# The first nine blocks of a fused attention and feed-forward kernel in an order written by hand, and its last addition by halves

## The chip, the cores and the metric

The kernel runs on one NeuronCore of a Trainium2 chip. Its engines are TensorE (PE in the profile, with its weight loads as PEld), VectorE (DVE), ScalarE (ACT), GpSimd (POOL) and SyncE (SP), which here only issues DMAs. The metric is the time of one execution on the device in microseconds; lower is better.

## The reference

With S = 2048 tokens, D = 576 columns, 32 heads of 18 columns and a hidden width of 4608, all in float32:

```
xn  = layernorm(x)
qkv = xn @ wqkv                      # 576 x 1728
# each token attends to itself and the tokens 2, 4, ..., 14 before it (W = 8, dilation 2)
A   = softmax(q . k / sqrt(18)) . v  # per head
out = x + A @ wo + relu(xn @ w1) @ w2
```

## The kernel before

**Layout.** The tokens are split into two phases (ph), even and odd ones, because a token only attends to tokens of its own parity. A phase has eight tiles (i = 0 to 7) of 128 tokens; two neighbouring tiles make a token block (tb = 0 to 3) of 256.

**Products.** A float32 product is made of three products in the PE's fast format. Each operand is split into a high part (`hi`, a rounded copy made by ACT) and a low part (`lo` = operand - `hi`, made by DVE). `two` (line 143) does this for weights, `transpose_split` (line 266) for the transposed, normalized x, and `h_mm` for the hidden layer. The list `TERMS` (line 294) holds the 14 products of one result: four of high x with high w1, four of low x with high w1, the mixed last 64 columns (one with high, one with low w1), and four of high x with low w1.

**Slots.** The feed-forward part runs over slots n = (phase, chunk of three hidden blocks c, token block tb, hidden block f). `h_mm(n)` (line 467) makes one 128 x 256 piece of the hidden layer: 14 products, then the rectified high part by ACT (L476) and the low part by DVE (L477). `o_mm(n)` (line 482) multiplies it with w2: 12 products into two accumulators `po`, one for each tile; after the third block of a chunk DVE adds them onto x (L500), which is also where the result is kept until `done` (line 458) stores it. The main loop (line 579) runs `h_mm` two slots (`LAG`) ahead of `o_mm`.

**Loads and splits of weights.** `split_task` puts a load and a split into the deque `tasks`. `stage_more` (line 128) issues the load on SP into a buffer of the pool `stp` (four buffers), at most three ahead; `run_splits(n)` makes the splits due by slot n, in order, and each one lets the next load go. `HEADW` gives the slots at which the first three blocks of w1 and of w2 are due. SP issues its DMAs in order, and one that waits for a buffer holds up those behind it.

**The opening.** 24 transposes of the identity (`WARM`, line 104) occupy PE from the start. For every tile, `stats` (line 239) makes mean and variance on DVE (L245 to L247) and, on POOL, the negated mean `nm` (L249) and the reciprocal standard deviation `rstd` (L250). `norm` (line 254) makes `xn`, in one pass on DVE (L261) or, with `act`, in two on ACT (L258, L259); ACT then copies the last 64 columns a second time (L263), so that one transpose of 128 columns puts them on both halves of the partitions. `make_xt` (line 285) has PE transpose a tile (L275 four times, L276 once) and ACT and DVE split it into `xT` (L278 to L281). The table `HEAD` says after which slot the steps for tiles 2 to 7 are put. Each engine executes its instructions in the order in which they are written here, so this table and the loop set the queues of ACT and DVE.

**The middle.** The products for q, k and v (`qkv_tile`), the attention on DVE (queued in `bg` and taken in by `run_bg` as an estimate of DVE's and PE's progress, `t`, allows), and the product with wo (`wo_a` to `wo_b`) are woven into the slots. `UNIT0` = 7 is the slot of the first `qkv_tile`; the five parts of wq for it are split in slots 2 to 6.

**The end.** After the last `o_mm`, DVE adds each of the two accumulators onto its tile of 576 columns, and SP stores the two tiles.

Of the kernel before, what the change touches and what calls it, by code (L numbers as in the profile page):

```python
# [33 lines left out]
HEAD = (  # L34
    (-2, 0, 'stats', 3),
    (-2, 1, 'xt', 2, True),
    (-1, 0, 'stats', 4),
    (-1, 1, 'norm', 3, True),
    (0, 0, 'xt', 3, False),
    (0, 0, 'norm', 4, True),  # L40
    (0, 0, 'stats', 6),
    (0, 1, 'stats', 5),
    (1, 1, 'norm', 5, False),
    (1, 1, 'xt', 4, False),
    (2, 1, 'xt', 5, False),
    (2, 1, 'norm', 6, True),
    (2, 1, 'stats', 7),
    (4, 0, 'norm', 7, True),
    (4, 1, 'xt', 6, False),
    (5, 1, 'xt', 7, False),  # L50
)
HALO = ((0, 112), (112, 127))
WARM = 24
# [3 lines left out]
def tile_body(ctx: ExitStack, tc: tile.TileContext, x, wqkv, wo, w1, w2, out):  # L57
    nc = tc.nc
    S, D = x.shape
# [5 lines left out]
    KT = 4  # L65
    DR = D - KT * P
    D2 = D // 2
    scale = Dh ** -0.5
# [4 lines left out]
    pool = lambda name, bufs, **k: ctx.enter_context(tc.tile_pool(name=name, bufs=bufs, **k))  # L73
# [20 lines left out]
    f32 = lambda ap: ap.bitcast(F32)  # L94
# [18 lines left out]
    def mm(o, l, r, start, stop, n):  # L113
        nc.tensor.matmul(o, l, r, start=start, stop=stop)  # L114
        t["pe"] += n / 2400.0 + 0.002

    def dve(n):
        t["dve"] += (n + 130) / 960.0
# [16 lines left out]
    def run_splits(n):  # L135
        while staged and staged[0][0] <= n:
            _, split, st = staged.popleft()
            split(st)
            stage_more()

    held = None

    def two(hi, lo, src, n):
        def rest():
            nc.vector.tensor_tensor(lo, src, f32(hi), op=ALU.subtract)  # L145
            dve(n)

        nc.scalar.activation(hi, src, AF.Copy)  # L148
        if held is None:
            rest()  # L150
        else:
            held.append(rest)

    W1, W2, WQ, WO = {}, {}, {}, {}

# [83 lines left out]
    def stats(ph, i):  # L239
# [4 lines left out]
        for h in range(2):  # L244
            nc.vector.bn_stats(st[:, h, :], xt[:, h * D2 : (h + 1) * D2])  # L245
        nc.vector.bn_aggr(mv, st)
        nc.vector.tensor_scalar(mv[:, 1:2], mv[:, 1:2], EPS, None, op0=ALU.add)  # L247
        nm = smp.tile([P, 1], F32, name="nm", bufs=4)
        nc.gpsimd.tensor_scalar(nm, mv[:, 0:1], -1.0, None, op0=ALU.mult)  # L249
        nc.gpsimd.tensor_tensor(r, mv[:, 1:2], mhalf, op=ALU.pow)  # L250
        MR[ph, i] = nm, r
        dve(700)

    def norm(ph, i, act=False):
        nm, r = MR.pop((ph, i))
        xn = tmp.tile([P, 640], F32, name="xn", bufs=3)
        if act:
            nc.scalar.activation(xn[:, 0:D], X[ph, i], AF.Identity, bias=nm)  # L258
            nc.scalar.activation(xn[:, 0:D], xn[:, 0:D], AF.Copy, scale=r)  # L259
        else:  # L260
            nc.vector.tensor_scalar(xn[:, 0:D], X[ph, i], nm, r, op0=ALU.add, op1=ALU.mult)  # L261
# [4 lines left out]
    def transpose_split(src, last, hi, mix, lo, free=False):  # L266

        if free:
            pa, pb = (ps_o.tile([P, 2, 512], F32, name="po")[:, 0, :] for _ in range(2))
            pa, pb = pa.rearrange("p (k c) -> p k c", k=KT), pb[:, 0:P]  # L270
        else:
            pa = ps_m.tile([P, KT, P], F32, name="pm")
            pb = ps_m.tile([P, P], F32, name="pm")
        for k in range(KT):
            nc.tensor.transpose(pa[:, k, :], src[:, k * P : (k + 1) * P], ident)  # L275
        nc.tensor.transpose(pb, last, ident)  # L276
        t["pe"] += 5 * 0.06
        nc.scalar.activation(hi, pa, AF.Copy)  # L278
        nc.vector.tensor_tensor(lo, pa, f32(hi), op=ALU.subtract)
        nc.scalar.activation(mix, pb, AF.Copy)  # L280
        nc.vector.tensor_tensor(mix[DR:P], pb[DR:P], f32(mix[DR:P]), op=ALU.subtract)  # L281
        dve(512)
        dve(128)

    def make_xt(ph, i, free=False):
# [5 lines left out]
        transpose_split(xn[:, 0:512], xn[:, 512:640], d[:, 0:4, :], d[:, 4, :], d[:, 5:9, :], free)  # L291
# [175 lines left out]
    def h_mm(n):  # L467
        ph, c, tb, f = slots[n]
        w, xt = W1[ph, c, f], XT[ph, tb]
        pt = ps_h.tile([P, TBN], F32, name="ph")  # L470
        for j, (a, b) in enumerate(TERMS):
            wb = w[:, b // 5, (b % 5) * P : (b % 5 + 1) * P]
            mm(pt, wb, xt[:, a, :], j == 0, j == len(TERMS) - 1, TBN)
        hi = hp.tile([P, TBN], F32R, name="hhi")
        lo = hp.tile([P, TBN], F32R, name="hlo")
        nc.scalar.activation(hi, pt, AF.Relu)  # L476
        nc.vector.scalar_tensor_tensor(lo, pt, 0.0, f32(hi), op0=ALU.max, op1=ALU.subtract)  # L477
        t["dve"] = max(t["dve"], t["pe"] + 0.6)
        dve(TBN)
        H[n] = (hi, lo)  # L480

    def o_mm(n):
        ph, c, tb, f = slots[n]
        hi, lo = H.pop(n)
        w = W2[ph, c, f]
        for k in range(2):
# [3 lines left out]
            for j, (l, b) in enumerate(((hi, 0), (hi, 1), (lo, 0))):  # L490
                for h in range(2):
                    mm(
                        PO[k][:, h, 0:D2], l[:, cs], w[:, b, h * D2 : (h + 1) * D2],
                        f == 0 and j == 0, f == C - 1 and j == 2, D2,
                    )
        if f == C - 1:
            for k in range(2):
                i = 2 * tb + k
                acc = X[ph, i].rearrange("p (h c) -> p h c", h=2)
                nc.vector.tensor_tensor(acc, PO[k][:, :, 0:D2], acc, op=ALU.add)  # L500
                dve(D)
                if c == NCH - 1:
                    done(ph, i)


    todo = {}
# [50 lines left out]
    for i in range(1, AHEAD + 1):  # L557
        stage_more(i)
        load_x(0, 1 + i)
    for i in range(AHEAD + 2, NI):  # L560
        load_x(0, i)
    stats(0, 0)
    stats(0, 1)
    held = []
    run_splits(-5)
    norm(0, 0)
    norm(0, 1)
    stats(0, 2)
    make_xt(0, 0)
    make_xt(0, 1, True)  # L570
    for f in held:
        f()
    held = None
    run_splits(-LAG)
    norm(0, 2, True)
    for z, k, op, *a in HEAD:
        (late if k else at)(z, {"stats": stats, "norm": norm, "xt": make_xt}[op], 0, *a)
    M = (3.0, 1.5, 3.0)
    for n in range(-LAG, len(slots)):
        run_splits(n)  # L580
# [37 lines left out]
```

## Time and profile before

| | |
|---|---|
| median of three runs | 1184.16 us (1183.68 to 1187.38) |
| the profiled execution | 1184.46 us, of which the profile's span is 1182.7 us |
| mean granted clock of PE | 0.998 |
| busy time of DVE | 822.3 us (70%) |
| busy time of ACT | 306.9 us (26%) |
| busy time of POOL | 40.1 us (3%) |
| moved by DMA | 86.16 MB, mean 73 GB/s |

The span runs from the first to the last instruction of the profiled execution. A group of instructions is given by its line, engine and operation, the tile it writes and those it reads, its shape and count; then its busy time and the mean of one, and the idle time of its engine just ahead of it with what ended that. In the timeline, the first number is the start and the second the busy time of a row of equal instructions (`x4` is four of them). Matmuls overlap each other, so the pitch between them is shorter than the duration of one. L12 is line 12 of the kernel.

### The profile page before, as it was taken

Reading aid. Unit: us, or ns where it says so; the run is one execution under the profiler, and the core shown is the slowest. Engines: PE = TensorE matmul, PEld = TensorE weight load, DVE = VectorE, ACT = ScalarE, POOL = GpSimd, SP = SyncE. Lnnn points to the kernel's source line nnn. Section 1 sums busy time; section 2 is a strip of 40 time slices with the busy share of each in tenths; the row PEclk is TensorE's granted clock in tenths of the full one; section 3 lists DMA queues with packets and bytes.
Section 4 is the critical chain, followed back from the end, with each engine's and each line's share of the span. In section 5 each row is a group of like instructions: output and inputs, shape, how many; then the busy total and the mean of one; then the engine's idle time right before and its main releaser. Section 6 shows DMA issues by size and latency. Waiting matters only on the chain.

```text
span 1182.7 us, 21731 instructions
## 1 busy us (share of the span) xinstructions
PE 1174.6 (99%) x8936; PEld 1164.9 (98%) x8936; DVE 822.3 (70%) x1301; ACT 306.9 (26%) x758; POOL 40.1 (3%) x63
## 2 busy tenths in 40 slices
PE   8999999999999999999999999999999999999998
PEld 8999999999999999999999999999999999999998
DVE  7516885888687668877673288758777884787852
ACT  5422222131222211322233123121322222222210
POOL 2000000010000000000020000000100000000000
PEclk9999999999999999999999999999999999999999
DMA  5312121130312211356342122121302213114541
GB/s 174 85 32 79 39 84 47 47 108 1 99 45 58 65 55 44 104 112 148 105 131 74 47 55 80 32 77 27 98 21 80 70 43 89 47 30 110 115 100 60
DMA packets 137364, 86.16 MB, mean 73 GB/s; under 512 B 48832, under 2 KB 120768, under 8 KB 137264
## 3 DMA queue, kind: packets, MB, share of 16 engines
q1 hardware_dynamic: 134736, 76.58, 24.0%
q10 hardware_dynamic: 2528, 8.20, 2.4%
q8 instruction: 70, 1.15, 0.4%
q14 instruction: 30, 0.25, 0.1%
HBM read 66.58 MB, written 9.96 MB: 65 GB/s over the span
## 4 chain that ended last, share of the span: by engine, by line
PE 95%; DVE 2%; DMA 2%; ACT 0%; SPq 0%; issue 0%; POOL 0%; DVEq 0%; ACTq 0%
PE ph L114 37%; PE po L114 37%; PE pm L114 20%; DMA st<-in_w 1%; DMA xn<-turned 1%; PE pm L275 0%; DVE pr L382 0%; DMA turned<-tr 0%; DVE x L500 0%; DMA x<-in_x 0%; DVE pr L345 0%; SPq L424 0%; DVE w1t L145 0%; DVE w2t L145 0%; DVE bst L245 0%
## 5 line engine op out<-in xcount | busy, mean ns | idle before, releaser
L114 PE MATMUL ph<-xT,w1t 128*128 128x256 f32 x4032 | 513.0, 278 | 1.3 <-ACT xT L278 0.6
L114 PEld LDWEIGHTS ph<-xT,w1t 128*128 128x128 f32 x4032 | 491.9, 188 | 2.1 <-ACT xT L278 0.8
L114 PE MATMUL po<-w2t,hhi 128*128 128x288 f32 x2304 | 400.7, 296 | 0.6 <-DVE w2t L145 0.3
L114 PEld LDWEIGHTS po<-w2t,hhi 128*128 128x128 f32 x2304 | 336.9, 188 | 2.4 <-issue 0.5
L476 ACT ACTIVATE hhi<-ph 128x256 fp32r<-128x256 f32 x288 | 110.1, 382 | 553.5 <-PE ph L114 538.2
L114 PE MATMUL po<-w2t,hlo 128*128 128x288 f32 x1152 | 244.7, 293 | 0.0
L477 DVE SCALAR_TENSOR_TENSOR hlo<-ph,hhi 128x256 fp32r<-128x256 f32 x288 | 121.5, 422 | 161.0 <-ACT hhi L476 160.1
L500 DVE TENSOR_TENSOR x<-po,x 128x576 f32<-128x576 f32 x192 | 143.4, 756 | 69.9 <-PE po L114 67.0
L114 PE MATMUL pm<-wq,xT 128*128 128x432 f32 x896 | 185.5, 358 | 0.0
L114 PEld LDWEIGHTS po<-w2t,hlo 128*128 128x128 f32 x1152 | 183.6, 188 | 0.0
L114 PEld LDWEIGHTS pm<-wq,xT 128*128 128x128 f32 x896 | 163.8, 188 | 5.6
L145 DVE TENSOR_TENSOR w2t<-st,w2t 128x576 fp32r<-128x576 f32 x72 | 54.3, 755 | 45.6 <-ACT w2t L148 45.4
L345 DVE TENSOR_TENSOR pr<-qo,k 128x1152 f32<-128x1152 f32 x64 | 85.8, 1349 | 0.0
L348 DVE TENSOR_REDUCE lg<-pr 128x64 f32<-128x1152 f32 x64 | 84.9, 1343 | 0.0
L375 DVE TENSOR_TENSOR pr<-lg,v 128x1152 f32<-128x1152 f32 x64 | 84.7, 1350 | 0.2
L382 DVE TENSOR_TENSOR pr<-pr 128x288 f32<-128x288 f32 (+1 forms) x128 | 70.6, 601 | 0.1
L145 DVE TENSOR_TENSOR w1t<-st,w1t 128x640 fp32r<-128x640 f32 x72 | 59.0, 820 | 13.8 <-ACT w1t L148 13.7
L148 ACT ACTIVATE w2t<-st 128x576 fp32r<-128x576 f32 x72 | 49.1, 683 | 57.2 <-PE po L114 42.4
L314 ACT ACTIVATE k<-pm 128x144 f32<-128x144 f32 x64 | 18.6, 291 | 143.9 <-PE pm L114 143.9
L148 ACT ACTIVATE w1t<-st 128x640 fp32r<-128x640 f32 x72 | 53.0, 736 | 11.4 <-DMA st<-in_w 11.4
L351 POOL TENSOR_SCALAR_AFFINE_SELECT lg<-lg 1x512 f32<-1x512 f32 x8 | 9.4, 1171 | 844.1 <-DVE lg L348 844.1
L114 PE MATMUL pm<-wq,oT 128*128 128x288 f32 x224 | 35.2, 296 | 0.3 <-ACT oT L438 0.3
(61 smaller groups left out, 444.7 us busy)
## 6 DMA issues: line engine op xcount, KB each, us to landing
st<-in_w SPq DMA_DIRECT2D x72, 288.0 KB, 3.0
st<-in_w SPq DMA_DIRECT2D x72, 256.0 KB, 3.0
st<-in_wqkv SPq DMA_DIRECT2D x32, 216.0 KB, 3.0
turned<-tr SPq DMA_DIRECT2D x64, 80.0 KB, 2.3
xn<-turned SPq DMA_DIRECT2D x16, 320.0 KB, 3.2
st<-in_w SPq DMA_DIRECT2D x144, 32.0 KB, 2.7
out<-x SPq DMA_DIRECT2D x16, 288.0 KB, 2.1
x<-in_x SPq DMA_DIRECT2D x15, 288.0 KB, 3.6
```

The costliest lines, as they stand in the source:

```text
L114: nc.tensor.matmul(o, l, r, start=start, stop=stop)
L145: nc.vector.tensor_tensor(lo, src, f32(hi), op=ALU.subtract)
L148: nc.scalar.activation(hi, src, AF.Copy)
L314: nc.scalar.activation(k[:, W - 1 + i, :], pq[:, 1, :], AF.Copy)
L345: nc.vector.tensor_tensor(pr[i], q, window(k, i), op=ALU.mult)
L348: nc.vector.tensor_reduce(lg[:, i], pr.pop(i).rearrange(heads, d=Dh), axis=AX.X, op=ALU.add)
L351: nc.gpsimd.affine_select(out=z, in_=z, pattern=[[1, NI], [1, W], [0, HG]], compare_op=ALU.is_ge, fill=-1e9 / scale, base=1 - W, channel_m ...
L375: nc.vector.tensor_tensor(pr[i].rearrange(heads, d=Dh), e, window(v, i).rearrange(heads, d=Dh), op=ALU.mult)
L382: nc.vector.tensor_tensor(o, z[:, 0:n], z[:, n : 2 * n], op=ALU.add)
L476: nc.scalar.activation(hi, pt, AF.Relu)
L477: nc.vector.scalar_tensor_tensor(lo, pt, 0.0, f32(hi), op0=ALU.max, op1=ALU.subtract)
L500: nc.vector.tensor_tensor(acc, PO[k][:, :, 0:D2], acc, op=ALU.add)
```

## The change

The slots 0 to 3 of `o_mm` and 0 to 5 of `h_mm`, with all steps of tiles 0 to 5, are no longer made by the loop and the table `HEAD` but written out one after another; the loop begins at slot `FIRST` = 4. To that end `stats`, `transpose_split`, `h_mm` and `o_mm` can be called in parts. In detail:

- All splits of the first w1 and w2 blocks are placed ahead of token block 1. The three second products (`o_mm`) of token block 0 are made before `h_mm` of block 1 (`o_mm(0)`, `o_mm(1)`, tile 3's transposes, `o_mm(2)`, then `h_mm(3)`). `h_mm(0)` and `h_mm(1)` are interleaved by terms.
- SP's order of loads: w1 block 1 and 2 stand ahead of x 3, and the three blocks of w2 ahead of x 4 to 7. `stp` has five buffers instead of four.
- The low parts of the first two blocks of w1 and of the five parts of the first wq are made by POOL (`by_pool`) instead of DVE.
- Tile 0 is normalized by ACT, tiles 1 to 5 by DVE (before: 0, 1 and 5 by DVE, 2 to 4 by ACT). Tiles 6 and 7 stay on ACT.
- The last 64 columns are no longer copied twice, in either phase: PE transposes 64 columns, and DVE reads the same 64 rows again for the low part.
- In the last slot, each accumulator is filled one half of the columns after the other, DVE adds it in two halves of 288 columns, and each half is stored by a DMA of its own, from SP and ACT in turn.

```
-HEADW = (-5, -2, -1, 0, 0, 1)
+HEADW = (-9, -8, -7, -6, -5, -4)
+FIRST = 4
 HEAD = (
...
+    (4, 0, 'stats', 6),
+    (4, 1, 'norm', 6, True),
+    (4, 1, 'stats', 7),
+    (5, 0, 'norm', 7, True),
+    (5, 1, 'xt', 6),
+    (6, 0, 'xt', 7),
 )
...
-    stp = pool("stp", 4)
+    stp = pool("stp", 5)
...
     def two(hi, lo, src, n):
...
+        nc.scalar.activation(hi, src, AF.Copy)
+        if step_now in by_pool:
+            nc.gpsimd.tensor_tensor(lo, src, f32(hi), op=ALU.subtract)
+        else:
             nc.vector.tensor_tensor(lo, src, f32(hi), op=ALU.subtract)
             dve(n)
...
     def norm(ph, i, act=False):
...
-        nc.scalar.activation(xn[:, D:640], xn[:, KT * P : D], AF.Copy)
...
+        nc.tensor.transpose(pb, src[:, KT * P : D], ident)
...
+        def last_high():
+            nc.scalar.activation(mix[0:DR], pb, AF.Copy)
+
+        def last_low():
+            nc.vector.tensor_tensor(mix[DR:P], pb, f32(mix[0:DR]), op=ALU.subtract)
+            dve(128)
...
     def o_mm(n, out=True):
...
+            if end:
+                terms.sort(key=lambda z: z[3])
...
+    def o_out(n, which=range(2)):
...
+            for h in range(2):
+                nc.vector.tensor_tensor(acc[:, h], PO[k][:, h, 0:D2], acc[:, h], op=ALU.add)
+                (nc.scalar if h else nc.sync).dma_start(o_v[ph, i][:, h * D2 : (h + 1) * D2], acc[:, h])
...
+    by_pool.update((-9, -8, *range(UNIT0 - 5, UNIT0)))
+    both, x_low, w_low, last = TERMS[0:4], TERMS[4:8], TERMS[9:13], [TERMS[8], TERMS[13]]
     load_x(0, 0, 2)
     load_x(0, 1)
...
+    stage_more(1)
+    load_x(0, 2)
+    stage_more(4)
+    load_x(0, 3)
+    stage_more(5)
+    stats(0, 0)
+    norm(0, 0, True)
+    stats(0, 1)
+    norm(0, 1)
+    x0 = make_xt(0, 0, parts=True)
+    x0[0]()
+    run_splits(-9)
+    x1 = make_xt(0, 1, bank=ps_o, parts=True)
+    x1[0]()
+    x0[1]()
+    x1[1]()
+    h_terms(0, both)
+    run_splits(-8)
+    stage_more(4)
+    for i in range(4, NI):
         load_x(0, i)
...
+    stats(0, 2)
+    for z in x0[2:], x1[2:]:
+        for f in z:
+            f()
+    h_terms(0, x_low)
+    h_terms(1, both)
+    h_terms(1, x_low)
+    h_terms(0, w_low + last)
+    h_terms(1, w_low + last)
+    run_splits(-7)
+    norm(0, 2)
+    h_out(0)
+    run_splits(-6)
+    h_terms(2, TERMS, True)
+    h_out(1)
+    stats(0, 3)
     run_splits(-5)
...
+    h_out(2)
+    x2 = make_xt(0, 2, bank=ps_h, parts=True)
+    x2[0]()
+    x2[2]()
+    norm(0, 3)
+    run_splits(-4)
+    x2[1]()
+    x2[3]()
+    o_mm(0)
+    o_mm(1)
+    make_xt(0, 3, bank=ps_h)
+    o_mm(2, out=False)
+    stats(0, 4)
+    stats(0, 5)
+    h_mm(3)
+    norm(0, 4)
+    norm(0, 5)
+    h_terms(4, TERMS)
+    h4 = h_out(4, parts=True)
+    h4[0]()
+    o_out(2, (0,))
+    make_xt(0, 4)
+    o_out(2, (1,))
+    h4[1]()
+    h_terms(5, TERMS)
+    h5 = h_out(5, parts=True)
+    h5[0]()
+    make_xt(0, 5)
+    h5[1]()
+    o_mm(3)
...
-    for n in range(-LAG, len(slots)):
+    for n in range(FIRST, len(slots)):
```

In this, `h_terms(n, terms)` makes the named products of `h_mm(n)`, `h_out(n)` its high and low part, `o_out(n)` the additions of `o_mm(n)`; `make_xt(..., parts=True)` returns the four steps high, low, high of the last 64, low of the last 64 (`x0[0]` to `x0[3]`).

More of the change, by code (lines that the diff above doesn't have):

```diff
@@ L264, in norm, with transpose_split @@
         XN[ph, i] = xn
[L266 to L270, printed above, removed]
+    def transpose_split(src, hi, mix, lo, bank=None, parts=False):
+        if bank is ps_o:
+            po = ps_o.tile([P, 2, 512], F32, name="po")
+            pa, pb = po[:, 0, :].rearrange("p (k c) -> p k c", k=KT), po[0:DR, 1, 0:P]
@@ L286, in make_xt @@
+        def last_low():
+            nc.vector.tensor_tensor(mix[DR:P], pb, f32(mix[0:DR]), op=ALU.subtract)
+            dve(128)
+        steps = high, low, last_high, last_low
+        if not parts:
+            for f in steps:
+                f()
+        return steps
+    def make_xt(ph, i, bank=None, parts=False):
         tb, h = divmod(i, 2)
@@ L465, in tile_body, with h_terms, h_out, high @@
     H, PO = {}, {}
-    def h_mm(n):
+    HP, HN = {}, {}
+    def h_terms(n, terms, other=False):
         ph, c, tb, f = slots[n]
         w, xt = W1[ph, c, f], XT[ph, tb]
-        pt = ps_h.tile([P, TBN], F32, name="ph")
-        for j, (a, b) in enumerate(TERMS):
+        if n not in HP:
+            HP[n] = ps_m.tile([P, TBN], F32, name="pm") if other else ps_h.tile([P, TBN], F32, name="ph")
+            HN[n] = 0
+        for a, b in terms:
             wb = w[:, b // 5, (b % 5) * P : (b % 5 + 1) * P]
-            mm(pt, wb, xt[:, a, :], j == 0, j == len(TERMS) - 1, TBN)
+            HN[n] += 1
+            mm(HP[n], wb, xt[:, a, :], HN[n] == 1, HN[n] == len(TERMS), TBN)
+    def h_out(n, parts=False):
+        pt = HP.pop(n)
         hi = hp.tile([P, TBN], F32R, name="hhi")
         lo = hp.tile([P, TBN], F32R, name="hlo")
[L476 to L479, printed above, removed]
         H[n] = (hi, lo)
-    def o_mm(n):
+        def high():
+            nc.scalar.activation(hi, pt, AF.Relu)
+        def low():
+            nc.vector.scalar_tensor_tensor(lo, pt, 0.0, f32(hi), op0=ALU.max, op1=ALU.subtract)
+            t["dve"] = max(t["dve"], t["pe"] + 0.6)
+            dve(TBN)
+        if not parts:
+            high()
+            low()
+        return high, low
+    def h_mm(n):
+        h_terms(n, TERMS)
+        h_out(n)
+    def o_mm(n, out=True):
         ph, c, tb, f = slots[n]
@@ L485, in o_mm @@
         w = W2[ph, c, f]
+        end = n == len(slots) - 1
         for k in range(2):
```

122 lines of the change are left out of this document (49 added, 73 removed).

## The prediction

> **What bounds the kernel now.** I read the engines' busy time and the chain that ended last, on the page, and then the opening and the end, the only places where the change puts work in another order.
>
> ```profile
> PE 1174.6 (99%) x8936; PEld 1164.9 (98%) x8936; DVE 822.3 (70%) x1301; ACT 306.9 (26%) x758; POOL 40.1 (3%) x63
> ...
> PE 95%; DVE 2%; DMA 2%; ACT 0%; SPq 0%; issue 0%; POOL 0%; DVEq 0%; ACTq 0%
> ```
>
> TensorE (PE) works 99% of the span and is 95% of the chain. Little can be won in the middle; what counts is how much of PE's time at the two ends is not products. The chain in order of time gives the price of PE's work at full clock: one o_mm of 12 products, the five transposes of a tile (two rows), one h_mm of 14 products.
>
> ```profile
> 22.62 1.59 PE po L114 x12
> 24.21 0.44 PE pm L275 x4
> 24.65 0.11 PE pm L276
> 24.76 1.61 PE ph L114 x14
> ```
>
> The timeline (start, duration) gives two marks to count the opening between: the first transposes of tile 0, and h_mm(9), the first product of token block 3. From about there to the last slot every engine has the same order in both kernels, apart from some copies of ScalarE (ACT) that go away.
>
> ```profile
> 1.35 5.38 PE L105 MATMUL po<-ident 128*128 128x128 f32 x24 [1.35 <-POOL mhalf L99]
> 4.26 0.22 POOL L249 TENSOR_SCALAR nm<-mv 128x1 f32<-128x1 f32 x1 [2.92 <-DVE mv L246]
> 5.84 0.22 POOL L249 TENSOR_SCALAR nm<-mv 128x1 f32<-128x1 f32 x1 [0.75 <-DVE mv L246]
> 6.52 0.97 PE L275 MATMUL pm<-ident,xn 128*128 128x128 f32 x4
> 8.80 0.57 POOL L250 TENSOR_TENSOR rstd<-mv,mhalf 128x1 f32<-128x1 f32 x1
> ...
> 42.22 1.78 PE L114 MATMUL ph<-xT,w1t 128*128 128x256 f32 x14
> ```
>
> From 6.52 to 42.22 are 35.70 us. The work ahead of the second mark is nine h_mm, seven o_mm and the transposes of eight tiles, in both kernels: 9 x 1.61 + 7 x 1.59 + 8 x 0.55 = 30.0 us. So **5.7 us are lost in the opening**, the most that a new order can bring there. Part of it is the clock, as two windows show (length, then busy time of PE, its weight loads, VectorE (DVE), ACT and GpSimd (POOL), granted clock, DMA):
>
> ```profile
> 7.24:10.65 3.41, 2.09 (x14) 1.41 (x13) 3.25 (x9) 3.27 (x10) 0.75 (x2) 1.00 0.95 257
> 10.66:14.06 3.40, 3.40 (x16) 3.18 (x16) 2.16 (x5) 1.49 (x4) 0.00 (x0) 0.50 0.96 314
> ```
>
> PE was busy for 2.09 of 3.41 us, and the 3.40 us behind that ran at a granted clock of 0.50: half of it, 1.7 us, is lost. The other 4.0 us are waits.
>
> **The start, up to the first product.** The groups of instructions have the durations of all that follows (the number behind the comma is the mean of one in ns):
>
> ```profile
> L477 DVE SCALAR_TENSOR_TENSOR hlo<-ph,hhi 128x256 fp32r<-128x256 f32 x288 | 121.5, 422 | 161.0 <-ACT hhi L476 160.1
> L476 ACT ACTIVATE hhi<-ph 128x256 fp32r<-128x256 f32 x288 | 110.1, 382 | 553.5 <-PE ph L114 538.2 <-DMA k<-k 15.3
> L145 DVE TENSOR_TENSOR w1t<-st,w1t 128x640 fp32r<-128x640 f32 x72 | 59.0, 820 | 13.8 <-ACT w1t L148 13.7
> L145 DVE TENSOR_TENSOR w2t<-st,w2t 128x576 fp32r<-128x576 f32 x72 | 54.3, 755 | 45.6 <-ACT w2t L148 45.4
> L148 ACT ACTIVATE w1t<-st 128x640 fp32r<-128x640 f32 x72 | 53.0, 736 | 11.4 <-DMA st<-in_w 11.4
> L148 ACT ACTIVATE wq<-st 128x432 fp32r<-128x432 f32 (+1 forms) x50 | 29.1, 582 | 5.9 <-DMA st<-in_wo 3.2 <-DMA st<-in_wqkv 2.7
> L245 DVE BATCH_NORM_STATS2 bst<-x 128x6 f32<-128x288 f32 x32 | 13.1, 448 | 3.4 <-DMA x<-in_x 3.3
> L246 DVE BATCH_NORM_AGGREGATE mv<-bst 128x2 f32<-128x12 f32 x16 | 3.3, 209 | 0.6
> L247 DVE TENSOR_SCALAR mv<-mv 128x1 f32<-128x1 f32 x16 | 2.5, 154 | 0.6
> L249 POOL TENSOR_SCALAR nm<-mv 128x1 f32<-128x1 f32 x16 | 6.0, 372 | 166.3 <-DVE mv L246 166.3
> L258 ACT ACTIVATE xn<-x,nm 128x576 f32<-128x576 f32 x5 | 3.9, 775 | 0.0
> L261 DVE TENSOR_SCALAR xn<-x,nm,rstd 128x576 f32<-128x576 f32 x11 | 6.8, 621 | 0.9 <-POOL rstd L250 0.7
> L278 ACT ACTIVATE xT<-pm 128x512 fp32r<-128x512 f32 x14 | 8.3, 594 | 7.2 <-PE pm L275 7.1
> L279 DVE TENSOR_TENSOR xT<-pm,xT 128x512 fp32r<-128x512 f32 x14 | 9.6, 688 | 4.8 <-ACT xT L278 4.8
> L281 DVE TENSOR_TENSOR xT<-pm,xT 64x128 fp32r<-64x128 f32 x14 | 4.1, 295 | 0.4
> ```
>
> Tile 0's norm goes to ACT: from nm at 4.26 + 0.22 = 4.48, two passes (L258, and L259 over the same columns) of 0.78 end at 6.04. DVE would be quicker, but the warm-up transposes (1.35 + 5.38) hold PE until about 6.5, so it costs nothing; without that cover it would cost about 0.5. Tile 1: nm at 5.84 + 0.22, rstd 0.57 (the undisturbed row at 8.80), norm 0.62 on DVE, done at 7.25. Its transposes follow tile 0's at once and end near 7.9, since they no longer wait for the 64-column copies of L263. Then ACT stands in the way. It starts when tile 0's four transposes end (6.52 + 0.97 = 7.5) and does tile 0's high part, w1's, and tile 1's before the first product can go: 7.5 + 0.59 + 0.74 + 0.59 = 9.4. **PE idles 1.5 us**, and 0.2 more until tile 1's low part is there (9.4 + 0.69, against four products to do).
>
> **VectorE's queue.** From 9.4 on it holds, ahead of the transposes of tile 4: three low parts of 512 (0.688) and four of 64 rows (0.295), statistics of tiles 2 to 5 (2 x 0.448 + 0.209 + 0.154 = 1.26 each), one low part of w1 (0.82), three of w2 (0.755), four of h (0.422), norms of tiles 2 to 4 (0.62): 2.06 + 1.18 + 5.04 + 0.82 + 2.27 + 1.69 + 1.86 = 14.9, up to 24.3. Neighbours overlap a little:
>
> ```profile
> 28.43 0.60 ACT L278 ACTIVATE xT<-pm 128x512 fp32r<-128x512 f32 x1 [1.05 <-PE pm L275]
> 28.55 1.41 DVE L500 TENSOR_TENSOR x<-po,x 128x576 f32<-128x576 f32 x2
> ...
> 28.93 0.27 ACT L280 ACTIVATE xT<-pm 128x128 fp32r<-128x128 f32 x1
> ```
>
> Two adds of L500 take 1.41, where w2's low part over the same 576 columns takes 0.755 for one, and ACT's L280 starts 0.10 before L278 ends. Over some 18 such places on DVE that is up to 0.9, so the queue ends at 23.4 to 24.3. PE arrives there at 9.6 + 5 x 1.61 + 3 x 1.59 + 2 x 0.55 = 23.5 at full clock and waits 0 to 0.8; I take 0.4. The queue would be no shorter than before, had not two low parts of w1 (2 x 0.82) gone to POOL, since three norms (3 x 0.62) come to it from ACT.
>
> **POOL's low parts.** No run here shows a subtraction of this size on POOL. The bounds are its nearest rows:
>
> ```profile
> L306 POOL MEMSET k<- 1x1008 f32 x8 | 7.4, 931 | 0.0
> L351 POOL TENSOR_SCALAR_AFFINE_SELECT lg<-lg 1x512 f32<-1x512 f32 x8 | 9.4, 1171 | 844.1 <-DVE lg L348 844.1
> masks.py:199 POOL TENSOR_SCALAR_AFFINE_SELECT ident<-ident 128x128 f32<-128x128 f32 x1 | 0.3, 292 | 0.1
> ```
>
> The memset makes an element in 0.92 ns, the select in 2.29 (1171 for 512, 292 for 128). For 640 elements that is 0.59 to 1.46 us; a second input read behind the first would double the upper one to 2.9. I take 1.5, by the select, which reads and writes as this does. The first part (ACT is done with it at 8.8) is then ready at 10.3, the second at 11.8, while PE has 4 + 4 + 8 products to do before it needs them. nm and rstd of tile 2, queued behind on POOL, come at 12.6, about when DVE reaches that norm: cost 0. The five parts of wq (432 elements, 0.99 each) leave DVE too; the first three fill POOL for 3.0 us from the start of h_mm(6), and nm of tile 6 is wanted 1.61 + 0.38 + 0.42 + 1.10 = 3.5 after that start: 0.5 of cover.
>
> **The transposes of tile 7** wait for the buffer of tile 6's. From the end of h_mm(6): high and low of h (0.38 + 0.42), statistics (1.10), nm (0.37), norm 6 on ACT (1.55), wq's fourth high part (0.58), high of h (0.38), norm 7 (1.55), tile 6's high (0.59) and low (0.69) = 7.6; PE has two o_mm, two h_mm and one tile beside it, 6.95. A wait of 0.7, less ACT's four overlaps of 0.1: 0.3 taken, 0 to 0.7 possible.
>
> **The clock.** In the stretch that decided before, PE stood idle for 3.41 - 2.09 = 1.3 us. In the same stretch it will now be idle for the 1.5 us ahead of the first product, so I expect half clock in the next 3.4 us again. That costs 1.7, but brings PE to tile 4 behind the end of DVE's queue, so that of the 0.4 there 0.2 is left. The losses are 1.5 + 0.2 + 1.7 + 0.2 + 0.3 = 3.9 against 5.7: **the opening wins 1.8** (1.2 to 2.3 by the bounds of the two waits). The Trainium skill has another rule: by "TensorE: Matmul & The Clock Gate", Part 1, full clock is lost only after an idle window of some 3.4 us. PE never stood for that long here, so by that rule the clock would stay full, which is the first rival below; the rows above, half clock after a stretch with PE busy for 61%, disagree with it, and the rows decide.
>
> **What costs nothing:** the loads of x 4 to 7 stand on SyncE behind w2's third, which waits for POOL's first part, 10.3. One takes, from issue to landing,
>
> ```profile
> x<-in_x SPq DMA_DIRECT2D x15, 288.0 KB, 3.6
> ```
>
> and tile 4's statistics are 3.5 us ahead of the end of DVE's queue, at about 20: some 6 us of cover. The fifth staging buffer only lets w2's second load go before any split has freed one.
>
> **The end.** One last add behind the last product becomes two of 288, and the stores are halved:
>
> ```profile
> 1178.76 0.76 DVE x L500
> L453 DVE TENSOR_TENSOR x<-pm,x 128x288 f32<-128x288 f32 x32 | 13.1, 453 | 28.0 <-PE pm L114 28.0
> out<-x SPq DMA_DIRECT2D x16, 288.0 KB, 2.1
> ```
>
> In the built program the first half's add waits for the last product of the whole accumulator, not for its own half's, so nothing starts earlier. Two adds take 0.91, less their overlap, against 0.76. The last store has half the bytes; what that saves of 2.1 us no row shows, between nothing and, by bytes, 1.0. So -0.15 to +0.9. The two last stores share the engines, hence nearer to the lower end: **0.2 won**.
>
> **The sum.** The profiled execution took 1184.46 us (span 1182.7), 0.3 above the median of the runs, 1184.16. 1184.46 - 1.8 - 0.2 = 1182.5, by itself 1181.3 to 1183.4.
>
> **Rivals.** *Full clock.* If the throttle lets the next stretch run, the losses are 1.5 + 0.2 + 0.4 + 0.3 = 2.4: 3.3 won, 4.0 if both waits overlap away, 2.7 if rstd of tile 2 is held up by DVE, as here:
>
> ```profile
> 18.63 1.17 POOL L250 TENSOR_TENSOR rstd<-mv,mhalf 128x1 f32<-128x1 f32 x1
> ```
>
> (1.17 instead of 0.57, beside low parts of w2). With 0.2 to 0.9 for the end: 1181.6 to 1179.6, middle 1180.9. For it: the trace gives only one share after which the clock fell. Against: the new share is no higher. *POOL is the bound, slower.* The low parts take twice the select's rate, 2.9 us. nm and rstd of tile 2 come 2 x 1.4 = 2.8 later, and DVE's queue with them; three parts of wq take 5.9 instead of 3.0, so nm of tile 6 is 2.4 late. 1182.5 + 2.8 + 2.4 = 1187.7, less the 0.5 of waits that this swallows: 1187.2. It decides from about 2.2 us a part, where the opening's win is gone. Against: the select's rate; for: two inputs, and 1.5 leaves no cover at tile 2. *The written order stalls PE elsewhere*, by some 2 us: 1184.5, no change. Against: the covers above.
>
> **Chances.** Forecast 0.52, full clock 0.30, POOL 0.13, stalls elsewhere 0.05. A measurement of this kernel tells about 0.3%, 3.6 us: faster is below 1180.6, slower above 1187.7. Of full clock rather over half lies below 1180.6, if I allow for the range of its waits and for the runs' own spread: 0.18. Of POOL the dearer half lies above 1187.7: 0.07. The range, 1180.0 to 1186.0, leaves out some 8 in 100 below and 9 above.
>
> **What would show it.** Right: first product near 9.4; w1t on POOL near 1500 ns; a granted clock of 0.50 for 3.4 us before 15; short waits ahead of the transposes of tiles 4 and 7; h_mm(9) near 40.4. Wrong: w1t on POOL above 2.2 us, with tile 2's norm waiting for rstd; h_mm(9) at 42 or later; the last store landing more than 2.9 us (0.76 + 2.1) behind the last product.

## The result, and the profile after

The changed kernel takes 1181.72 us (median of 8 executions, 1181.18 to 1182.05), the kernel before 1184.80 beside it (8, 1183.68 to 1187.38). The ratio is 0.9971, with a 95% interval of 0.9962 to 0.9981: some 3 us are won, a small gain but clear of the noise. The forecast was 1182.5, range 1180.0 to 1186.0. The profiled execution took 1181.42 us.

Its page: the span, and the busy times (DVE 3.5 us less than before, ACT 5.0 less, POOL 7.4 more).

```profile
span 1179.7 us, 21695 instructions
PE 1171.0 (99%) x8936; PEld 1162.3 (99%) x8936; DVE 818.8 (69%) x1298; ACT 301.9 (26%) x738; POOL 47.5 (4%) x70
```

The opening, from the timeline of the changed kernel (start, busy time, engine, line; in brackets what ended the idle time). The lines have moved: L274 are the transposes, L105 all products, L260 the norm on DVE, L279 and L282 the high and the low part of a tile, L139 the low parts on POOL, L500 and L503 those of h.

```profile
6.16 0.66 PE L274 MATMUL pm<-ident,xn 128*128 128x128 f32 x4 [0.23 <-ACT xn L258]
7.08 0.58 DVE L260 TENSOR_SCALAR xn<-x,nm,rstd 128x576 f32<-128x576 f32 x1 [0.70 <-POOL rstd L245]
7.71 0.66 PE L274 MATMUL po<-ident,xn 128*128 128x128 f32 x4 [0.79 <-DVE xn L260]
8.51 0.60 ACT L279 ACTIVATE xT<-po 128x512 fp32r<-128x512 f32 x1 [0.44 <-PE po L275]
9.16 0.74 PE L105 MATMUL ph<-xT,w1t 128*128 128x256 f32 x4 [0.69 <-ACT xT L279]
...
12.82 1.82 PE L105 MATMUL pm<-xT,w1t 128*128 128x256 f32 x14
...
23.83 0.63 PE L274 MATMUL pm<-ident,xn 128*128 128x128 f32 x4 [0.17 <-DVE xn L260]
...
37.41 0.65 PE L274 MATMUL pm<-ident,xn 128*128 128x128 f32 x4 [0.48 <-DVE xT L282]
...
39.60 1.78 PE L105 MATMUL ph<-xT,w1t 128*128 128x256 f32 x14
```

h_mm(9), the row at 39.60, starts 2.62 us earlier than before (42.22). From the first transposes to there pass 33.44 us, so that 3.4 of it are lost, against 5.7 before; the first transposes are also 0.36 earlier. The loss is spread as follows, with the prediction's lengths of the pieces: 1.9 up to the first product (1.0 between the two tiles, 0.9 behind the second), 0.44 in the first 28 products (9.16 to 12.82), 0.3 up to tile 4, of which 0.17 is its wait, 0.7 from there to tile 7, of which 0.48 is its wait.

The windows of the changed kernel by the throttle's stretches (stretch, length, busy time of PE, PEld, DVE, ACT and POOL with their instructions, granted clock, DMA share, GB/s):

```profile
4.97:8.38 3.41, 2.40 (x19) 1.72 (x17) 2.36 (x6) 2.27 (x4) 1.05 (x4) 1.00 0.84 250
8.38:11.79 3.41, 2.72 (x21) 2.44 (x21) 2.52 (x8) 2.36 (x5) 3.29 (x4) 1.00 0.88 257
11.79:15.21 3.42, 3.42 (x32) 3.42 (x31) 3.26 (x7) 2.36 (x6) 0.32 (x1) 1.00 1.02 351
```

Full clock is granted from 4.97 on and stays: PE is busy for 2.40 of 3.41 us (70%) in the stretch ahead of the first product, where before it was 2.09 (61%) and the next stretch ran at half clock. The idle time there is no shorter (0.79 and 0.69 in two pieces), but the boundary at 8.38 cuts it in two. That this is why the clock stayed is not shown (see below).

The end, from the chain of waits of the changed kernel (start, length, what; DVEq is the sequencer of DVE):

```profile
1175.17 1.25 DVE x L550 x3
1176.42 0.36 DVEq L715
```

PE's last product ends at 1175.92 (before 1178.72), and the last store lands at 1178.68, 2.76 us behind it (before 1181.65, 2.93 behind).

### The profile page after: what moved, and what is told of

Its sections match the earlier page's. It is cut to its first block, busy times and chain, and to the rows that moved or that the text cites. A ratio compares the mean times of both kernels' runs of the same rounds, so it can differ in the third digit from the quotient of the medians.

```text
span 1179.7 us, 21695 instructions
## 1 busy us (share of the span) xinstructions
PE 1171.0 (99%) x8936; PEld 1162.3 (99%) x8936; DVE 818.8 (69%) x1298; ACT 301.9 (26%) x738; POOL 47.5 (4%) x70
## 4 chain that ended last, share of the span: by engine, by line
PE 96%; DVE 1%; DMA 1%; ACT 0%; issue 0%; POOL 0%; SPq 0%; DVEq 0%; ACTq 0%; POOLq 0%
PE ph L105 38%; PE po L105 38%; PE pm L105 20%; PE pm L274 0%; DVE bst L239 0%; DMA xn<-turned 0%; DMA x<-in_x 0%; DMA st<-in_wqkv 0%; DMA turned<-tr 0%; DVE pr L395 0%; POOL rstd L245 0%; DVE w2t L141 0%; ACT xn L257 0%; DVE hlo L503 0%; DVE x L550 0%
## 5 line engine op out<-in xcount | busy, mean ns | idle before, releaser
L105 PE MATMUL ph<-xT,w1t 128*128 128x256 f32 x4018 | 509.3, 278 | 0.7 <-ACT xT L279 0.7
L105 PEld LDWEIGHTS ph<-xT,w1t 128*128 128x128 f32 x4018 | 489.1, 188 | 1.1 <-ACT xT L279 1.0
L105 PE MATMUL po<-w2t,hhi 128*128 128x288 f32 x2304 | 400.7, 296 | 0.0
L105 PEld LDWEIGHTS po<-w2t,hhi 128*128 128x128 f32 x2304 | 337.0, 188 | 1.0
L500 ACT ACTIVATE hhi<-ph 128x256 fp32r<-128x256 f32 x287 | 109.9, 383 | 583.4 <-PE ph L105 560.2
L105 PE MATMUL po<-w2t,hlo 128*128 128x288 f32 x1152 | 245.0, 293 | 0.0
L503 DVE SCALAR_TENSOR_TENSOR hlo<-ph,hhi 128x256 fp32r<-128x256 f32 x287 | 120.8, 421 | 169.2 <-ACT hhi L500 168.5
L105 PE MATMUL pm<-wq,xT 128*128 128x432 f32 x896 | 185.5, 358 | 0.0
L105 PEld LDWEIGHTS po<-w2t,hlo 128*128 128x128 f32 x1152 | 183.8, 188 | 0.0
L105 PEld LDWEIGHTS pm<-wq,xT 128*128 128x128 f32 x896 | 163.8, 188 | 5.6
L105 PE MATMUL pm<-wq,oT 128*128 128x288 f32 x224 | 35.2, 296 | 0.8 <-ACT oT L451 0.8
```

## The experiments

All were timed in five rounds beside the kernel before, four kernels to a chip. The three chips differ by up to 0.9 us in the kernel before, so ratios and neighbours on a chip are to be compared. An execution is listed with its mean granted clock: those with a stretch of half clock in the opening show 0.998 or 0.999, those without 1.0, at times 0.999.

| kernel | chip | median us (lowest to highest, n) | ratio to before, 95% interval | h_mm(9) starts |
|---|---|---|---|---|
| before | a | 1183.85 (1182.65 to 1185.68, 33) | | 42.22 (first profile) |
| e1, end alone | a | 1184.66 (1182.32 to 1185.27, 11) | 1.0001 [0.9993, 1.0010] | 41.86 |
| e2, gap filled | a | 1184.11 (1183.39 to 1185.38, 11) | 1.0002 [0.9993, 1.0011] | 41.36 |
| e3, no POOL | a | 1181.56 (1181.02 to 1183.01, 11) | 0.9980 [0.9971, 0.9989] | 41.88 |
| e9, old end | a | 1181.53 (1181.16 to 1181.82, 11) | 0.9980 [0.9971, 0.9989] | 39.42 |
| before | b | 1184.77 (1183.30 to 1185.64, 28) | | |
| e12, changed, again | b | 1181.19 (1180.95 to 1181.27, 6) | 0.9970 [0.9959, 0.9982] | 39.76 |
| e13, h_mm(3) first | b | 1186.21 (1185.98 to 1187.86, 11) | 1.0015 [1.0006, 1.0024] | 46.12 |
| e11, x first | b | 1183.35 (1182.83 to 1185.15, 11) | 0.9993 [0.9983, 1.0002] | 41.42 |
| e4, norms by ACT | b | 1184.26 (1183.20 to 1184.97, 11) | 0.9997 [0.9988, 1.0005] | 41.65 |
| before | c | 1184.25 (1182.77 to 1186.17, 33) | | |
| e15, no POOL, old end | c | 1181.86 (1180.96 to 1183.57, 11) | 0.9983 [0.9974, 0.9992] | 42.01 |
| e8, two waits removed | c | 1182.10 (1181.58 to 1182.37, 11) | 0.9983 [0.9974, 0.9992] | 40.58 |
| e5, in turn | c | 1181.79 (1181.25 to 1182.30, 11) | 0.9980 [0.9972, 0.9989] | 40.33 |
| e16, copy put back | c | 1184.14 (1183.80 to 1184.23, 11) | 1.0001 [0.9992, 1.0010] | 43.05 |

### e12: the changed kernel once more

Nothing is edited; it stands beside the next three on one chip.

> The changed kernel once more, on the chip of the next three, so that they can be told from it by less than the chips differ: 1181.2 to 1182.1, full clock in most executions. If its first median, 1181.72, owed something to its chip: 1182.5 to 1183.5.

1181.19, 0.997 of the kernel before: the first measurement owed nothing to its chip.

### e1 and e9: the end by itself

e1 is the kernel before with the changed end, e9 the changed kernel with the old end.

```
# e1 (and the adds and stores by halves, as in the change)
+            if n == len(slots) - 1:
+                terms.sort(key=lambda z: z[3])
# e9
-        end = n == len(slots) - 1
+        end = False
...
-            if n < len(slots) - 1:
+            if True:
```

> The kernel before with the end by halves alone. If the end is worth what the trace of after shows (span 3.0 us shorter, h_mm(9) 2.6 us earlier, so 0.4 left for the end): 0.4 us under the kernel before, 1184.4 against 1184.8, and from the last product to the last landing 2.5 us instead of 2.9. If the halves bring nothing because both adds wait for the last product (0.2 or less, as I had it): within 0.2 of the kernel before, and the opening has all of the gain.

> The changed kernel with the old end (two adds of 576 columns, two whole stores). 0.4 us slower than the changed kernel, 1182.1, if the end is worth 0.4 in it; 1181.7 if it is worth nothing. The opening is the changed one: h_mm(9) at 39.6 if the profiled execution has full clock from the start, otherwise up to 1.6 later.

Neither time can be told from that of its neighbour without the edit. The traces are sharper than the times: in all four traces with the old end the last store lands 2.93 to 2.95 us behind the last product, in nine of ten with the new one 2.74 to 2.78, in the tenth 3.16. The end wins 0.2, as forecast, and in the way forecast: both half-adds of the second accumulator stand behind its last product.

### e2: the gap filled

The kernel before with ten transposes of the identity, five ahead of the first product and five behind the fourth.

```
+        if n == 0:
+            FILL.append(ps_h.tile([P, TBN], F32, name="ph"))
+            fill(5)
...
+            if n == 0 and j == 4:
+                fill(5)
```

> The kernel before with ten idle transposes on PE in its two longest gaps of the opening (five ahead of the first product, five behind the first four products), so that PE is busy for about 90% instead of 61% of the stretch ahead of the half clock; no other engine changes. If the share of busy time decides the clock: granted clock 1.00 from 10 to 15 us, h_mm(9) 0.5 to 1.5 us earlier, 1183.3 to 1184.2. If the clock's fall was only a matter of the phase in that execution, or if the waits of VectorE hide it anyway: 1184.8, the same as before, with a 0.50 stretch still seen in some executions.

Full clock came: 8 of 11 executions show 1.0, where the kernel before on this chip has 10 of 33. The time did not move. The timeline of e2 shows why:

```profile
17.39 0.52 PE L114 MATMUL po<-w2t,hhi 128*128 128x288 f32 x2
18.53 0.53 PE L114 MATMUL po<-w2t,hhi 128*128 128x288 f32 x2 [0.62 <-DVE w2t L145]
...
17.71 1.43 DVE L145 TENSOR_TENSOR w2t<-st,w2t 128x576 fp32r<-128x576 f32 x2
```

o_mm(0) starts 1.24 earlier than before (18.63), and then waits for DVE, which reaches the low part of w2 only 0.9 earlier than before (18.61); at h_mm(9) 0.86 is left. In the kernel before DVE's queue is the next bound behind the clock. The rest of the 0.86 can't be seen in the time: within single executions, waits far behind the opening differ by as much (below). e2 does not give the price of the clock either: its eight executions with 1.0 took 1184.08 on the mean, the ten of the kernel before on this chip 1183.11. Whether the filling costs that 1 us is not known.

### e3 and e15: without POOL

e3 is the changed kernel with all low parts on DVE; e15 the same with the old end besides.

```
-    by_pool.update((-9, -8, *range(UNIT0 - 5, UNIT0)))
+    by_pool.clear()
```

> The changed kernel with all low parts back on VectorE (POOL makes none). If VectorE's queue is the bound of the opening, two low parts of w1 (1.6 us) lie on the way to the first products and to the transposes of tile 4: 1.2 to 2.2 us slower than the changed kernel, about 1183.4, and still under the kernel before. If VectorE has slack there: within 0.4 of the changed kernel, and POOL was not needed. If POOL's parts are what the whole change lives on: back at 1184.8.

> The changed kernel with two parts undone at once: no low part on POOL, and the old end. If each is worth nothing, as e3 and e9 showed one by one: 1181.0 to 1181.9, a ratio to the kernel before of 0.997 to 0.998. If they hide each other (DVE, with two more low parts of w1, reaches tile 4 so much later that only a cheaper end hid it): 1182.3 or more.

By the medians POOL's parts are worth nothing. By the executions they are worth something: of the 22 of e3 and e15, 7 took 1182.62 to 1183.57, with a clock of 0.999, while the other 15 took 1180.96 to 1181.91; of the 25 of the changed kernel (two chips) and e9 none took more than 1182.05. Both profiled ones fell among the slower; here the timeline of e3, and its window:

```profile
9.21 0.74 PE L105 MATMUL ph<-xT,w1t 128*128 128x256 f32 x4 [0.95 <-ACT xT L279]
10.78 4.48 PE L105 MATMUL ph<-xT,w1t 128*128 128x256 f32 x24 [0.83 <-DVE xT L282]
...
7.11:10.52 3.41, 1.89 (x13) 1.18 (x11) 2.14 (x4) 2.48 (x5) 0.00 (x0) 1.00 0.79 221
10.52:13.93 3.41, 3.15 (x14) 3.15 (x15) 3.28 (x10) 0.90 (x2) 0.75 (x2) 0.50 0.96 303
```

With w1's low part on DVE, tile 0's stands behind it, PE stops a second time behind its fourth product, and the stretch has 1.89 us of work (55%): half clock follows, and 24 products take 4.48. The means with and without it are 1182.82 and 1181.41 in e3, 1183.25 and 1181.64 in e15: it costs 1.4 to 1.6.

### e13: the order of the products

Three lines are moved: tile 3's transposes and `h_mm(3)` stand ahead of the three `o_mm`.

```
+    make_xt(0, 3, bank=ps_h)
+    h_mm(3)
     o_mm(0)
     o_mm(1)
-    make_xt(0, 3, bank=ps_h)
     o_mm(2, out=False)
     stats(0, 4)
     stats(0, 5)
-    h_mm(3)
```

> The changed kernel, with h_mm(3) and tile 3's transposes ahead of o_mm(0), o_mm(1) and o_mm(2). Theory A (the order of the products carries the gain: the three o_mm fill the time in which DVE and POOL prepare tile 3): PE stands from 14.9 until norm 3 is done on DVE at 17.4, and again for tile 3's high and low part; h_mm(3) starts near 18.9 instead of after 4.8 us of o_mm, and o_mm(0) behind it near 20.5. Of some 3.4 us of idle PE about 0.3 comes back at tile 4: 1184.5 to 1185.2. Theory B (the gain is the full clock and what was taken off DVE, the order is free): within 0.5 of the changed kernel, 1181.3 to 1182.3.

5.0 us over e12, and slower than the kernel before: with h_mm(3) first, the rest of the change wins nothing. The timeline and windows of e13:

```profile
18.22 1.12 PE L274 MATMUL pm<-ident,xn 128*128 128x128 f32 x4 [2.97 <-DVE xn L260]
20.02 3.35 PE L105 MATMUL ph<-xT,w1t 128*128 128x256 f32 x14 [0.47 <-ACT xT L279]
...
14.79:18.20 3.41, 0.46 (x5) 0.19 (x3) 3.21 (x10) 1.66 (x5) 1.23 (x2) 1.00 1.02 351
18.20:21.62 3.42, 2.92 (x12) 2.47 (x13) 2.49 (x5) 0.75 (x2) 0.00 (x0) 0.50 0.61 173
21.62:25.03 3.41, 3.41 (x17) 3.41 (x16) 1.16 (x4) 0.38 (x1) 0.00 (x0) 0.50 0.04 11
```

PE stands for 2.97 us until norm 3 and for 0.47 until tile 3's high part, as theory A had it, which gave 2.8 to 3.5 over the 1181.7 known then. What is beyond it is the clock, which neither theory counted: behind the empty stretch h_mm(3) takes 3.16 (20.02 to 23.18) instead of 1.61. The profiled execution (mean clock 0.997, 1187.86) has two stretches of half clock with 6.33 us of busy PE, half of which is lost; with the 3.4 of waits these are 6.6 of the 6.8 by which it lies above the profiled e12. The nine executions with 0.998 or 0.999 took 1185.98 to 1186.36.

### e11 and e4: the order of the loads, and who normalizes

e11 puts w2's second and third load behind x 4 to 7; e4 gives the norms of tiles 2, 3 and 4 back to ACT.

```
# e11
-    stage_more(5)
...
-    run_splits(-8)
-    stage_more(4)
     for i in range(4, NI):
         load_x(0, i)
+    run_splits(-8)
+    stage_more(4)
# e4 (and so for tiles 3 and 4)
-    norm(0, 2)
+    norm(0, 2, True)
```

> The changed kernel, with the loads of x 4 to 7 ahead of w2's second and third load, as before the change. Theory A (the early w2 loads are what makes the early o_mm possible): four loads of 288 KB stand in front, so that w2's second block lands 2 to 4 us later than its 14.1; o_mm(1), which starts at 16.4, and o_mm(2) wait for DVE's low parts by 1.5 to 2.5 us: 1183.2 to 1184.2. Theory B (the loads are hidden, or share the engines either way): 1181.3 to 1182.2.

> The changed kernel, with tiles 2, 3 and 4 normalized by ACT in two passes of 0.78, as before the change. Theory A (ACT stands in the way of w2's high parts and of tile 3 when it does the norms): three norms add 4.7 us to ACT and take 1.7 from DVE; w2's parts come 0.3 to 0.5 late for o_mm(0) and o_mm(2), norm 4 ends 0.2 later than DVE's: 1182.2 to 1183.0. Theory B (DVE's queue decides, as the prediction had it for tile 4): DVE has 1.7 us less, the wait of 0.2 to 0.5 ahead of tile 4 goes: 1181.2 to 1181.6.

e11 lost 2.2 against e12, within theory A. Its timeline shows ACT waiting for the load for 3.31 us, and o_mm(1) behind it:

```profile
16.98 0.68 ACT L137 ACTIVATE w2t<-st 128x576 fp32r<-128x576 f32 x1 [3.31 <-DMA st<-in_w]
...
17.72 0.53 PE L105 MATMUL po<-w2t,hhi 128*128 128x288 f32 x2 [0.82 <-ACT w2t L137]
18.51 0.53 PE L105 MATMUL po<-w2t,hhi 128*128 128x288 f32 x2 [0.26 <-DVE w2t L141]
```

e4 lost 3.1, more than twice what theory A expected (0.5 to 1.3 over 1181.7), and theory B is out: DVE had 1.7 us less to do and yet came later, since its queue waits for ACT's high parts. The timeline of e4:

```profile
13.40 0.78 ACT L258 ACTIVATE xn<-xn,rstd 128x576 f32<-128x576 f32 x1
14.08 0.36 ACT L500 ACTIVATE hhi<-ph 128x256 fp32r<-128x256 f32 x1
...
14.48 0.42 DVE L503 SCALAR_TENSOR_TENSOR hlo<-ph,hhi 128x256 fp32r<-128x256 f32 x1 [2.07 <-ACT hhi L500]
...
19.85 0.76 DVE L141 TENSOR_TENSOR w2t<-st,w2t 128x576 fp32r<-128x576 f32 x1 [1.52 <-ACT w2t L137]
```

The second pass of norm 2 holds the high part of h_mm(0) until 14.08 (in e12 12.22). DVE is idle for 2.07 us ahead of h's low part and for 1.52 ahead of w2's third. At h_mm(9) PE is 1.9 later than in e12, by waits for w2 and for tile 4. The two profiled executions are 3.2 apart: 0.8 more is a longer wait at 1095 (below), and some 0.4 was not found.

### e16: the copy of the last 64 columns

The changed kernel with the copy of the kernel before and transposes of 128 columns, for all tiles.

```
+        nc.scalar.activation(xn[:, D:640], xn[:, KT * P : D], AF.Copy)
...
-        nc.tensor.transpose(pb, src[:, KT * P : D], ident)
+        nc.tensor.transpose(pb, src[:, KT * P : 640], ident)
```

> The changed kernel with the copy of the last 64 columns by ACT and transposes of 128 columns put back, for all tiles. Theory A (ACT stands in the way at the start): tile 1's copy waits for its norm on DVE, 7.66, and holds up ACT's three high parts behind it: first product at 7.9 + 3 x 0.62 = 9.75 instead of 9.16, 0.6 lost, and 0.26 more on ACT ahead of tiles 4 and 5: 0.6 to 1.2 over e15. Theory B (the copies hide behind tile 1's norm and the order later has slack): within 0.3 of e15.

2.3 over e15, more than theory A expected. The first product is 0.36 later than the changed kernel's, not 0.6, but the cost is at tiles 2 and 3. The timeline of e16:

```profile
7.62 0.26 ACT L262 ACTIVATE xn<-xn 128x64 f32<-128x64 f32 x1 [1.21 <-DVE xn L260]
...
14.09 0.26 ACT L262 ACTIVATE xn<-xn 128x64 f32<-128x64 f32 x1 [2.96 <-DVE xn L260]
14.25 0.37 ACT L501 ACTIVATE hhi<-ph 128x256 fp32r<-128x256 f32 x1
```

The copy of 0.26 us waits for the norm on DVE, and the high part of h_mm(0), ready behind its products for over a microsecond, stands behind it: ACT is idle for 2.96. That delays the low parts of h and of w2, and each `o_mm` then waits 0.26 to 0.32 for w2; tiles 4 and 7 wait 0.64 and 1.13. The prediction counted the copies at tiles 0 and 1 only.

### e5: the products in turn

```
     h_terms(0, x_low)
+    h_terms(0, w_low + last)
     h_terms(1, both)
     h_terms(1, x_low)
-    h_terms(0, w_low + last)
     h_terms(1, w_low + last)
```

> The changed kernel with all 14 products of h_mm(0) ahead of those of h_mm(1), instead of interleaved by terms. Theory A (interleaving hides the low parts that come late): the product with tile 0's mixed rows would come 12 products behind the first, at 9.16 + 12 x 0.115 = 10.5, but DVE makes that part at 11.4: 0.9 of idle PE, of which up to 0.3 comes back at tile 4: 0.6 to 0.9 over e15. Theory B (the later waits take it in): within 0.3 of e15.

The wait is there, 0.46 at the mixed rows of tile 0, and h_mm(9) starts 0.7 later than in the changed kernel. The median shows none of it, 0.1 under e15; its interval, some 1 us wide to either side, can't rule out 0.7. e15's median holds four executions with half clock; against the other seven (mean 1181.64) e5's mean of 1181.78 is 0.1 later.

```profile
11.60 2.09 PE L105 MATMUL ph<-xT,w1t 128*128 128x256 f32 x16 [0.46 <-DVE xT L289]
```

### e8: two of the waits that are left

The changed kernel with x 1 loaded in two halves, and the norms of tiles 6 and 7 on DVE.

```
-    load_x(0, 1)
+    load_x(0, 1, 2)
...
-    (4, 1, 'norm', 6, True),
+    (4, 1, 'norm', 6),
...
-    (5, 0, 'norm', 7, True),
+    (5, 0, 'norm', 7),
```

> The changed kernel with tile 1 of x loaded in two halves, so that its statistics start earlier, and the norms of tiles 6 and 7 made by DVE in 0.6 instead of by ACT in 1.55. Theory A (the waits that the trace still shows are worth their length): the 0.48 ahead of tile 7's transposes goes, and 0 to 0.4 of the 0.9 between the transposes of tiles 0 and 1: 0.5 to 0.9 under e15, 1180.4 to 1181.1. Theory B (behind each the next thing is late by as much: ACT's three high parts ahead of the first product, DVE's queue at tile 7): within 0.3 of e15.

Nothing was won: against e15's executions at full clock (mean 1181.64) e8's median is 0.5 later. The timeline of e8 shows both parts at work:

```profile
8.79 3.74 PE L105 MATMUL ph<-xT,w1t 128*128 128x256 f32 x28 [0.69 <-ACT xT L279]
...
34.95 1.13 POOL L139 TENSOR_TENSOR wq<-st,wq 128x432 fp32r<-128x432 f32 x1
35.02 1.37 DVE L260 TENSOR_SCALAR xn<-x,nm,rstd 128x576 f32<-128x576 f32 x1 [0.44 <-POOL rstd L245]
38.38 0.66 PE L274 MATMUL pm<-ident,xn 128*128 128x128 f32 x4 [1.72 <-DVE xT L282]
```

The first product starts at 8.79 instead of 9.16, and 0.26 of this is still there at tile 4. But norm 7 takes 1.37 us on DVE instead of 0.58: it starts 0.07 behind a low part of wq on POOL. Two adds (1.41 together) and tile 6's low part stand behind it, and the wait ahead of tile 7's transposes grows from 0.48 to 1.72. Halves for x 1 alone, or the norms on DVE without POOL's parts, were not run, so no version here beats the changed kernel.

## Why the prediction was right

**The time** came out 0.8 below the forecast, well within the range: 3.1 won where 2.0 were forecast. The reasons agree less well than the number.

**The clock: wrong.** The prediction expected half clock for 3.4 us ahead of 15, for 1.7. It came in neither trace of the changed kernel, and the times of its 14 executions, 1180.95 to 1182.05, leave no room for it. The step that failed is "In the same stretch it will now be idle for the 1.5 us". In the profiled execution the boundary left 1.01 of idle time in one stretch and 0.69 in the next; in e12 the wait ahead of the first product was one piece of 0.97. Where the stretches lie relative to the kernel is not fixed either: full clock began at 4.09 to 7.32 in the fourteen traces. Which of the two kept the clock up stays open. In the profiled execution, 3.41 us from 5.80 on would have had PE busy for only 1.71; in e12 PE is busy for at least 2.44 of any 3.41 us from 2 us on. The condition of the first rival, full clock, is what happened; its own sum (3.3 won in the opening) was too high by 1.0, counted from the same start.

**The start: too small a term.** 1.9 were lost up to the first product, not 1.5, though it started at 9.16, near the 9.4 expected. The sum itself was off: it counted the idle time from 7.9 on, but by the prediction's own marks, 6.52 and 9.4, less 1.1 for two tiles, 1.8 are lost. In the profiled execution it is not ACT's queue that decides but tile 1's chain, as the waits of PE in the changed kernel show:

```profile
PE po L274 <- DVE xn L260: 0.8, 1, 0.8
PE ph L105 <- ACT xT L279: 0.7, 1, 0.7
PE pm L274 <- DVE xT L282: 0.5, 1, 0.5
```

Tile 1 of x landed at 5.10, so norm 1 was done at 7.66 instead of 7.25. In e12, where it landed at 4.78, tile 1 followed tile 0 at once and ACT's three high parts decided; the first product started at 9.12 all the same. Two chains end there together. Counted from e12's first transposes (6.53), 1.5 are lost there and 3.2 up to h_mm(9), so part of the 0.4 hangs on the execution.

**The first 28 products** lost 0.44, not 0.2. **Tile 4's wait** was 0.17 (forecast 0.2 behind half clock, 0.4 at full clock), **tile 7's** 0.48 (0.3 taken, 0 to 0.7 possible). Some 0.4 of loss in small pieces stand in no term. So the losses without the clock were 3.4, where the terms gave 2.2 to 2.4, and the clock's 1.7 fell away: an error of 1 and one of 1.7 the other way. That is why the opening won 2.3, plus 0.36 by an earlier start, and not 1.8. That the time came so near to the forecast is in part luck. The earlier start, too, belongs to that execution: its 24 warm-up transposes took 4.58, with full clock from 4.97 on, but 5.38 before and in e12; there the first transposes began at 6.52 and 6.53.

**POOL: right.** The groups of the changed kernel on POOL (busy time, mean ns of one):

```profile
L139 POOL TENSOR_TENSOR w1t<-st,w1t 128x640 fp32r<-128x640 f32 x2 | 3.1, 1557 | 1.2 <-ACT w1t L137 1.1
L139 POOL TENSOR_TENSOR wq<-st,wq 128x432 fp32r<-128x432 f32 x5 | 5.5, 1120 | 6.6 <-ACT wq L137 6.6
```

1557 ns against 1500 taken by the select's rate; wq's 1120 against 990. The second rival, POOL as the bound, needed 2.2 us a part. That POOL's parts also keep PE's start together (e3) was in no step.

**The end: right**, 0.17 to 0.2 in the traces.

**What carries the gain.** Taken back one at a time, the order of the products costs 5.0 (some 3.4 of it waits, the rest the half clock behind them), the norms on DVE 3.1, the dropped copy 2.3, the early w2 loads 2.2, and the whole change is worth 3.1: they are not terms of a sum, since each needs the others. The clock is the smaller part. On the three chips the kernel before takes, on the mean, 1183.11, 1184.25 and 1183.72 in executions with a clock of 1.0, and 1184.74, 1185.26 and 1185.26 in those with 0.998. Without any half clock the change is then worth 1.6 (e9, with the old end), 3.1 (e12) and 2.1 (e15, with the old end and without POOL); that it escapes the half clock adds 0.4 to 0.8, by which the mean of all executions before lies above its 1.0 group.

**What stays open** is where single executions differ by up to 1 us behind the opening. One place is the product with wo near 1093, which waits for a DMA's data by way of ACT; PE's waits behind the opening, in the changed kernel and in the kernel before:

```profile
PE pm L105 <- ACT oT L451: 0.8, 1, 0.8
```

```profile
PE pm L114 <- ACT oT L438: 0.3, 1, 0.3
```

It is 0.83 here, 0.26 before, 0.30 in e12, 1.06 in e4 and under 0.1 in e16. So 0.7 at h_mm(9) (e5) can't be read from one profile's span.

## What to carry to other kernels

Where engines take their instructions in order, look for the short one that waits for another engine: a copy of 0.26 us cost 2.3 us by what stood behind it. Fill the time in which the next tile is prepared with products that are ready, and have their weights loaded by then; either without the other gave back most of the gain (e11) or all of it (e13). In a sum of idle pieces leave a term for the small ones, and price a clock that hangs on where a stretch's boundary falls as a chance over executions.

## What the runs showed of the hardware

**The clock's stretches have a free phase.** In the four traces with half clock it lasted for one or two stretches of 3.41 us, and full clock began anywhere from 4.09 to 7.32 us of the span in the fourteen traces. PE's busy time in a stretch does not tell what follows. Full clock fell behind stretches with PE busy for 0.46 (e13), 1.81 (e15), 1.89 (e3) and 2.09 us (before). It stayed behind 2.08 (e5) and 2.13 (e4, e9), but also behind 2.01 in e1 and 1.69 in e8:

```profile
6.01:9.42 3.41, 2.01 (x14) 1.28 (x12) 2.80 (x10) 2.26 (x7) 1.37 (x4) 1.00 0.97 285
...
36.15:39.56 3.41, 1.69 (x15) 1.50 (x14) 2.88 (x6) 0.91 (x3) 2.85 (x3) 1.00 0.51 124
39.56:42.97 3.41, 3.41 (x27) 3.39 (x27) 1.92 (x4) 1.27 (x4) 0.00 (x0) 1.00 0.25 77
```

The first row is of e1, the other two of e8, where PE stood for half of the stretch, 1.72 us of it in one piece, and the next one still ran at full clock. So no bound on the busy time that the profile gives fits all of these; what else decides is open. The Trainium skill, "TensorE: Matmul & The Clock Gate", Part 1, has the window free-running, with 3413 ns, and the traces agree. Its other rule there, that full clock is lost after an idle window, the traces contradict: the loss came with PE busy for 55 and 61%.

**DVE and POOL slow each other.** In e8 a norm beside a low part on POOL took 1.37 us instead of 0.58, and on POOL `rstd` took 1.04 instead of 0.57 beside a low part of w2 on DVE, in the changed kernel:

```profile
15.55 0.77 DVE L141 TENSOR_TENSOR w2t<-st,w2t 128x576 fp32r<-128x576 f32 x1
15.71 1.04 POOL L245 TENSOR_TENSOR rstd<-mv,mhalf 128x1 f32<-128x1 f32 x1
```

DVE's adds from the accumulators were not slowed: two took 1.41 in e8 beside POOL, as before. The Trainium skill, "GPSIMD Engine Reference", "1. Specifications", names interfaces to SBUF that are shared with VectorE; that the norm is among the forms that collide, e8 shows. The kernel before has such a norm as well: at 618.84 it takes 1.05, beside a memset on POOL.
